# Windowed attention with sinks and an MLP on one Trainium2 core: moving four casts and pairing the sink products

## The chip, the core and the metric

The kernel runs on one core of one Trainium2 chip. A core has TensorE (PE, matrix products), VectorE (DVE), ScalarE (ACT), GpSimd (POOL) and SyncE (SP, which only issues transfers here). All five run their own instruction lists in order and wait for one another by semaphores. The metric is device time in microseconds; lower is better. Before the change the median of four runs is 217.16 us (216.92 to 217.25).

## What is computed

Attention over 4 batches of 8 heads, 768 tokens, 64 elements a head, in which a token sees the first four tokens (the sinks) and the last 128; then an MLP with the activation h * sigmoid(1.702 h).

```python
scores = scale * np.matmul(q, k.transpose(0, 1, 3, 2))
is_sink = pos[None, :] < 4
in_window = (rel >= 0) & (rel < 128)
a = softmax(np.where(is_sink | in_window, scores, -1e9))
x = (a @ v).transpose(0, 2, 1, 3).reshape(3072, 512)
h = x @ w_in                     # w_in 512 x 2048
out = (h * (1.0 / (1.0 + np.exp(-1.702 * h)))) @ w_out
```

All inputs and the output are float32; the kernel multiplies in float16.

## The kernel before

**Tiling.** The 3072 tokens are 12 blocks of 256, numbered k = 0 to 11; a batch is three blocks, r = k mod 3. A block is two halves (j) of 128 tokens. The 8 heads are 4 pairs p; i is the head in its pair. Blocks with r > 0 also see the block before them and the sinks.

**Stages of a block.** `load` (L403) brings q, k and v by transfers and casts them to float16 in pieces by `copy` (L294, so all casts and copies have the line L295). `turn` (L506) transposes q and k into `blkT`: blocks 0 to 3 on PE (L542), from block 4 on by a transposing transfer that SP issues (L564). `scores` (L572) multiplies: a group of one pair (blocks 0 and 1) or two pairs (later), each head in a PSUM bank of its own; the first group of a block with r > 0 also makes the scores of the sinks for all four pairs in one more bank (L594). So a group takes 2 to 5 of the 8 banks. In blocks 0 and 1 a matmul with the identity (L606) puts the mask under the scores. ACT takes exps (L639 for the window into `at`, L626 for the sinks into `ats`), DVE multiplies by the mask from block 2 on (L646). `back` (L657) multiplies by v (L679) and leaves sums and products in a bank; v carries a column of ones, so a head has 65 columns. DVE takes reciprocals (L697, rcp) and scales (L701, xn), and x is transposed into `xT`, on PE in blocks 0 to 2 (L725, with a copy by L295), by SP's transfer later (L713). `mm1` (L738) makes the first product of the MLP in 8 steps of two 128-column chunks (L752), each step with tanh on ACT (L764) and one combining instruction on DVE (L766). The second product is L781 in blocks 0 and 1; later blocks use a form with seven block products instead of eight (L947, in the last block L873), for which DVE and POOL make sums and differences of g (L847) and, once, of the weights (L826).

**Who sets the order.** Nothing is ordered by hand. Every step is an `Op` with the engines that may run it, a duration the author assumed, a priority (smaller is more urgent) and the PSUM banks it takes. `Plan.run` (L76) simulates all engines with these and at each step places the operation that can start first, the more urgent one if several can start within 20 ns. The lists that come out are the instruction order of each engine. Priorities follow a nominal timetable, `nominal(k, slot)` (L387), of 17.3 us a block in 8 slots. A step that several engines may run goes to the one that would end it first.

**Around the change.** In `Plan.run`, L122 to L134: an operation that takes more than two banks and can't have them yet sets `held_from`, and operations that take banks and would start after that are put off, so that the waiting group gets its banks. L126 applies only to groups of three banks or more. The casts of v are allowed by `CAST_V` (L363): block 1's may go to POOL, DVE or ACT, blocks 2 and 3's to POOL, from block 4 on to ACT (L366); their priority is `nominal(k - 1, -4)` (L482), for block 1 the value 350. The casts of q and k (L449 to L452) are eight a block from block 4 on, each 64 x 512, all on POOL. In block 0 reciprocal and scaling have the priority -2245 for pair 2 and 2080 for pair 3 (L698, L708), and the copy of the transposed x -1380 and 2945 (L732).

In `av` (L669) the sink product comes first in each head's group of products:

```python
for i in range(2):
    mms = [(As[:, bass.ts(j, P)], vs16[:, b, p, i])] if r else []
    mms += [(A[:, i, c : c + P], src[:, jj, 2 * p + i]) for src, jj, c in blocks]
    for n, (a_, v_) in enumerate(mms):
        nc.tensor.matmul(avp()[:, j, i], a_, v_, start=(n == 0), stop=(n == len(mms) - 1))
```

`As` holds the exps of the sinks of all heads, and `vs16` the sinks' v with zeros in the rows of the other heads; so both heads of a pair have the same left operand there.

Of the kernel before, what the change touches and what calls it, by code (L numbers as in the profile page):

```python
# [14 lines left out]
P = 128  # L15
# [45 lines left out]
class Plan:  # L61
# [14 lines left out]
    def run(self, warm=None, warm_until=0.0, late_bank=0.0):  # L76
# [39 lines left out]
        while todo:  # L116
            best = None
            for e in ENGINES:
                found = sorted(
                    [(*could(o, e), o) for o in ready[e]], key=lambda x: (x[2].prio, x[2].seq)  # L120
                )
                keep, held_from = [], None  # L122
                for s0, s, o in found:
                    if s0 is None:
                        continue
                    if o.acq and o.acq[1] > 2 and (s is None or s > s0):  # L126

                        held_from = s0 if held_from is None else min(held_from, s0)
                        if s is not None:
                            keep.append((s, o))  # L130
                        continue
                    if s is None or (o.acq and held_from is not None and s >= held_from):
                        continue
                    keep.append((s, o))  # L134
                if not keep:
                    continue
                first = min(s for s, _ in keep)
                s, o = min(((s, o) for s, o in keep if s <= first + 20), key=lambda x: (x[1].prio, x[1].seq))
                lat = o.engs[e][1]
                key = s if len(o.engs) == 1 else s + lat - min(x[1] for x in o.engs.values())  # L140
                if best is None or key < best[0]:
                    best = (key, s, o, e)
            if best is None:
                raise RuntimeError("no operation can be planned")
            _, s, o, e = best
            dur, lat = o.engs[e]
            if e == "PE" and warm and s < warm_until:
                t = max(free["PE"], 400.0)
                while t + 300 < s:
                    order.append((t, -1, warm, e, None))  # L150
                    t += 400 if t < 4500 else 220
            for x in o.engs:
                ready[x].remove(o)
            o.eng, o.start = e, s
            if o.acq:
                cls, n = o.acq
                o.banks, o.places = [], []
                for _ in range(n):
                    b = min((b for b in bank_free if bank_free[b] <= s), key=lambda b: (bank_free[b], b))
                    del bank_free[b]  # L160
                    o.banks.append(b)
                    p = min((p for p in count[cls] if count[cls][p] <= s), key=lambda p: (count[cls][p], p))
                    del count[cls][p]
                    o.places.append(p)
            free[e] = s + dur
            if isinstance(lat, tuple):
                ns, nd = lat
                t = s + dur
                while sum(n * min(1.0, (b - t) / max(b - a, 1.0)) for a, b, n in ring[e] if b > t) + nd > RING:
                    t += 25  # L170
                free[e] = t
                soft = e == "POOL"
                begin = max(s + (2200 if soft else 1300), dma_free[soft])
                shared = max(0.0, min(dma_free[not soft] - begin, ns))
                if shared:
                    dma_free[not soft] += shared
                dma_free[soft] = begin + ns + shared
                ring[e].append((begin, dma_free[soft], nd))
                landed[soft].append(dma_free[soft] + 900)
                o.end = dma_free[soft] + 900 + o.late  # L180
            else:
                o.end = s + lat
            for owner, i in o.rel:
                t = o.end + 80
                bank_free[owner.banks[i]] = t
                count[owner.acq[0]][owner.places[i]] = t
            for u in o.users:
                u.left -= 1
                if not u.left:
                    for x in u.engs:  # L190
                        ready[x].append(u)
            order.append((s, o.seq, o.fn, e, o))
            todo -= 1
# [9 lines left out]
def kernel(  # L203
# [11 lines left out]
    nc = tc.nc  # L215
# [6 lines left out]
    NK = B * R  # L222
# [9 lines left out]
    KS, LASTS = globals().get('OPT',{}).get('KS',2), globals().get('OPT',{}).get('LASTS',NK)  # L232
# [19 lines left out]
    vs16 = pool.tile([P, B, NP, 2, E], FP16, name="vs16")  # L252
# [25 lines left out]
    plan = Plan(8, {"m": 1, "s": 5, "t": 4, "a": 2, "x": 2, "h": RTH, "o": OPT_("NO", 3)})  # L278
# [9 lines left out]
    def cast(n, engs):  # L288

        ns = {"POOL": (n / 0.96 + OPT_("PC", 100), n / 0.96 + OPT_("PC", 100) + 100), "DVE": (n / 1.92 + 65, n / 1.92 + 165),  # L290
              "ACT": (n / 1.2 + 100, n / 1.2 + 210)}
        return {e: ns[e] for e in engs.split()}
# [18 lines left out]
    OPT = globals().get("OPT", {})  # L311
# [48 lines left out]

    OPT = globals().get("OPT", {})
    CAST_QK = ["DVE ACT", "POOL DVE"] + ["POOL"] * (NK - 2)
    CAST_V = ["POOL DVE ACT", OPT.get("V1", "POOL DVE ACT")] + ["POOL"] * (NK - 2)  # L363

    for k_ in range(OPT.get("VK", 4), NK):
        CAST_V[k_] = OPT.get("VA", "ACT")  # L366
# [20 lines left out]
    def nominal(k, slot):  # L387
        return 9000.0 + k * L + slot * L / 8
# [14 lines left out]
    def load(k):  # L403
        b, r = divmod(k, R)
        sl = k if k < RS else (k - 1) % (RS - 1)
        t0 = r * TB
        prio = load_at(f"a{k}")
        war = reuse("s32", sl) + ([o_m[k - 2, 0][-1]] if k > KT else [])
        dst, dv = qk32[sl], v32[sl]
        lq = {}  # L410
# [23 lines left out]
        def lv(dma, h):  # L434
# [3 lines left out]
                   prio=load_at("a1") + 1.5 + k / 8 if k < 2 else load_at(f"v{k}") if k == 2 else prio + 0.7, kind="load")]  # L438
# [4 lines left out]
        war = reuse("qk16", k % RQ)  # L443
        if k >= KT:
            C = slots(c16)
            for e in range(2):
                for j in range(2):
                    for i in range(2):
                        def f(eng, e=e, j=j, i=i):  # L449
                            copy(eng, C[64 * i : 64 * i + 64, e, :, j].rearrange("s p (h d) -> s p h d", h=2),  # L450
                                 dst[64 * j : 64 * j + 64, e, :, i].rearrange("s (p h) d -> s p h d", h=2))
                        o = plan.any(cast(512, "ACT" if k > KS and e == j and i < OPT.get("QA", 0) else CAST_QK[k]), f, lq[e] + war, prio=nominal(k - 1, -7), kind="cqk")  # L452
                        o_cqk[k, 2 * e + j, i] = o
        else:
            C = eights(c16)
            for h in range(2):
                for e in range(2):
                    def f(eng, e=e, h=h):
                        copy(eng, C[:, e, :, :, h].rearrange("s i a d -> s a i d"),
                             dst[:, e].rearrange("s h i d -> s (h i d)").rearrange("s (h a i d) -> s h a i d", h=2, a=4, i=2)[:, h])  # L460
                    o_cqk[k, e, h] = plan.any(cast(512, CAST_QK[k] if k != 1 else "DVE ACT" if e else OPT.get("Q1", "POOL")), f, [lq[e][h]] + war,
                                              prio=nominal(k - 1, -7 + 2 * h) if k else NEVER + h, kind="cqk")
# [3 lines left out]
        war = reuse("v16", k % RV)  # L466
# [4 lines left out]
        for n in range(parts):  # L471
            o_l = o_lv[0]
            got = []
            for j in range(2):
                for i in range(2):
# [3 lines left out]
                    if k < 2 and "DVE" in ns:  # L479
                        ns["DVE"] = (60 * w + 70, 60 * w + 170)  # L480
                    o = plan.any(ns, f, [o_l] + war + [o_ones],
                                 prio=(nominal(k - 1, -4) if k else NEVER + 5 + n), kind="cv")  # L482
# [174 lines left out]
    def back(k, p):  # L657

        b, r = divmod(k, R)
# [6 lines left out]
        def avp():  # L666
            return f32(o_a)[:, 0 : 4 * E].rearrange("s (j h e) -> s j h e", j=2, h=2)

        def av():  # L669
            for j in range(2):  # L670
                if r:
                    blocks = [[(vp, 1, 0), (vt, 0, P)], [(vt, 0, 2 * P), (vt, 1, 3 * P)]][j]
                else:
                    blocks = [[(vt, 0, 0)], [(vt, 0, P), (vt, 1, 2 * P)]][j]
                for i in range(2):
                    mms = [(As[:, bass.ts(j, P)], vs16[:, b, p, i])] if r else []
                    mms += [(A[:, i, c : c + P], src[:, jj, 2 * p + i]) for src, jj, c in blocks]
                    for n, (a_, v_) in enumerate(mms):
                        nc.tensor.matmul(avp()[:, j, i], a_, v_, start=(n == 0), stop=(n == len(mms) - 1))  # L679

        dur = 12 * 31 if r else 6 * 31
        deps = [*o_m[k, p], *o_cv[k, p]] + ([o_se[k], *o_cv[k - 1, p], o_vs[b]] if r else [])
        rc, X = rcp[u % RR], xn[u % RR]
        if k < KX:
# [1 line left out]
        else:  # L686
# [3 lines left out]
            war = []  # L690
# [422 lines left out]
```

## Time and profile before

| | |
|---|---|
| median of the runs | 217.16 us (216.92 to 217.25) |
| the profiled execution | 216.79 us, of which the span of instructions is 215.0 us |
| TensorE clock granted | 1.00 throughout |
| busy in the span | PE 206.8, DVE 172.1, ACT 146.1, POOL 100.2 us |
| casts of v on ACT | 38, of them 35 of 64 x 512, mean 619 ns |
| casts of q and k on POOL, 64 x 512 | 64, mean 646 ns |
| matmuls of L679 with `at` and `v` / with `ats` and `vs` | 352 / 128, all of 65 columns |

Times are us unless marked ns. "PE" is the matmul, "PEld" its weight load, which overlaps. A line of a group gives line, engine, operation, tiles (out<-in) and shapes, then busy time and the mean of one. In an order of time, the columns are start, length, engine, line and operation, and in brackets how long the engine stood before it and what ended that. A duration of a matmul holds its way through the array; the next one starts well before it ends, so the distance of starts tells what a matmul costs when they follow closely.

### The profile page before, as it was taken

Reading aid. Unit: us, or ns where it says so; the run is one execution under the profiler, and the core shown is the slowest. Engines: PE = TensorE matmul, PEld = TensorE weight load, DVE = VectorE, ACT = ScalarE, POOL = GpSimd, SP = SyncE. Lnnn points to the kernel's source line nnn. Section 1 sums busy time; section 2 is a strip of 40 time slices with the busy share of each in tenths; the row PEclk is TensorE's granted clock in tenths of the full one; section 3 lists DMA queues with packets and bytes.
Section 4 is the critical chain, followed back from the end, with each engine's and each line's share of the span. In section 5 each row is a group of like instructions: output and inputs, shape, how many; then the busy total and the mean of one; then the engine's idle time right before and its main releaser. Section 6 shows DMA issues by size and latency. Waiting matters only on the chain.

```text
span 215.0 us, 5827 instructions
## 1 busy us (share of the span) xinstructions
PE 206.8 (96%) x2290; PEld 166.6 (78%) x2290; DVE 172.1 (80%) x369; ACT 146.1 (68%) x290; POOL 100.2 (47%) x144
## 2 busy tenths in 40 slices
PE   7979999999999999999999999999999999999992
PEld 2447876676767878988988978988988988988881
DVE  3685777997779798889878989889878969978861
ACT  2699645957987768769696597679696566525530
POOL 3496437799862482196712393196702202203210
PEclk9999999999999999999999999999999999999999
DMA  5999999999959728989979729959894024024044
GB/s 183 352 234 204 207 304 210 324 297 283 206 128 224 190 49 125 266 163 281 173 157 214 198 54 194 267 137 272 162 147 102 3 51 98 0 56 94 0 99 99
DMA packets 65914, 36.58 MB, mean 170 GB/s; under 512 B 27968, under 2 KB 61120, under 8 KB 65888
## 3 DMA queue, kind: packets, MB, share of 16 engines
q1 hardware_dynamic: 60848, 30.19, 59.7%
q0 software_dynamic: 4592, 5.37, 13.2%
q10 hardware_dynamic: 448, 0.66, 1.0%
q8 instruction: 18, 0.29, 0.6%
q14 instruction: 8, 0.07, 0.1%
HBM read 27.56 MB, written 6.29 MB: 157 GB/s over the span
## 4 chain that ended last, share of the span: by engine, by line
PE 77%; DVE 11%; ACT 7%; issue 3%; ACTq 0%; DVEq 0%
PE bank L752 34%; PE bank L947 19%; PE bank L781 6%; PE bank L679 6%; PE bank L614 4%; DVE gT L766 3%; DVE gF L847 3%; ACT at L639 3%; PE bank L873 3%; PE bank L1061 3%; ACT v L295 2%; PE bank L542 2%; DVE xb L701 1%; DVE at L646 1%; ACT th L764 1%
## 5 line engine op out<-in xcount | busy, mean ns | idle before, releaser
L752 PE MATMUL bank<-xT,w_in 128*128 128x256 f16 x768 | 99.7, 273 | 0.4 <-DVE gT L766 0.4
L764 ACT ACTIVATE th<-bank 128x512 f16<-128x512 f32 x96 | 57.3, 601 | 40.9 <-PE bank L752 32.6
L752 PEld LDWEIGHTS <-w_in 128*128 128x128 f16 x768 | 72.0, 98 | 11.5 <-issue 2.5
L766 DVE SCALAR_TENSOR_TENSOR gT<-th,bank 128x512 f16<-128x512 f16 x96 | 65.3, 682 | 14.2 <-ACT th L764 12.4
L847 POOL TENSOR_TENSOR gT<-gT 128x512 f16<-128x512 f16 (+1 forms) x22 | 24.8, 1128 | 73.1 <-DVE gF L847 66.1
L639 ACT ACTIVATE at<-bank 128x512 f16<-128x512 f32 (+1 forms) x96 | 49.2, 571 | 6.1 <-PE bank L614 6.0
L295 POOL CAST qk<-qk 64x512 f16<-64x512 f32 (+1 forms) x70 | 44.9, 643 | 13.9 <-DMA qk<-in_q_dram 11.3
L947 PE MATMUL bank<-third,gF 128*128 128x256 f16 x144 | 34.1, 273 | 0.0
L947 PE MATMUL bank<-w_out,gT 128*128 128x256 f16 x144 | 34.0, 273 | 0.0
L947 PEld LDWEIGHTS <-gT 128*128 128x128 f16 x288 | 27.5, 98 | 4.1 <-issue 0.9
L646 DVE TENSOR_TENSOR at<-at,bank 128x1024 f16<-128x1024 f16 (+1 forms) x40 | 25.4, 637 | 6.2 <-ACT at L639 6.0
L947 PE MATMUL bank<-wf,gT 128*128 128x256 f16 x144 | 27.0, 272 | 0.0
L295 ACT CAST v<-v 64x512 f16<-64x512 f32 (+1 forms) x38 | 22.9, 603 | 1.0 <-DMA v<-in_v_dram 0.3
L947 PEld LDWEIGHTS <-gF 128*128 128x128 f16 x216 | 21.1, 98 | 2.6 <-DVE gF L847 0.2
L679 PE MATMUL bank<-v,at 128*128 128x65 f16 x352 | 21.2, 193 | 0.6 <-DVE at L646 0.3
L679 PEld LDWEIGHTS <-at 128*128 128x128 f16 x352 | 17.6, 97 | 1.6 <-DVE at L646 0.5
L947 PE MATMUL bank<-w_out,gF 128*128 128x256 f16 x72 | 17.2, 273 | 0.0
L781 PE MATMUL bank<-w_out,gT 128*128 128x512 f16 x64 | 15.9, 379 | 0.0
L701 DVE TENSOR_TENSOR xb<-bank,rcp 128x256 f16<-128x256 f32 x36 | 15.0, 417 | 0.4
L679 PE MATMUL bank<-vs,ats 128*128 128x65 f16 x128 | 14.9, 193 | 0.1
L847 DVE TENSOR_TENSOR gF<-gT,gF 128x512 f16<-128x512 f16 (+1 forms) x22 | 14.1, 639 | 0.3
L614 PEld LDWEIGHTS <-blkT 64*128 64x128 f16 x256 | 8.0, 94 | 8.0 <-issue 6.2
(75 smaller groups left out, 208.9 us busy)
## 6 DMA issues: line engine op xcount, KB each, us to landing
out_dram<-osb SPq DMA_DIRECT2D x46, 128.0 KB, 2.4
v<-in_v_dram SPq DMA_DIRECT2D x11, 512.0 KB, 6.6
qk<-in_q_dram SPq DMA_DIRECT2D x8, 512.0 KB, 4.6
qk<-in_k_dram SPq DMA_DIRECT2D x8, 512.0 KB, 6.0
w_in<-in_moe_w_in_dram POOLq DMA_DIRECT2D x4, 512.0 KB, 9.3
w_out<-in_moe_w_out_dram POOLq DMA_DIRECT2D x4, 512.0 KB, 12.4
qk<-in_q_dram SPq DMA_DIRECT2D x6, 256.0 KB, 5.1
qk<-in_k_dram SPq DMA_DIRECT2D x4, 256.0 KB, 4.9
```

Source lines behind the costliest of these rows:

```text
L295: {"POOL": nc.gpsimd.tensor_copy, "DVE": nc.vector.tensor_copy, "ACT": nc.scalar.copy}[e](out=out, in_=in_)
L614: nc.tensor.matmul(f32(o_s, 2 * n + i)[:, c : c + w], src[d, j], Q[d].rearrange("d j s -> d (j s)")[:, q0 : q0 + w], start=k >= KM, stop=T ...
L639: nc.scalar.activation(out=A[:, i, 0:W], in_=f32(o_s, 2 * n + i)[:, 0:W], func=AF.Exp, scale=scale)
L646: nc.vector.tensor_tensor(out=A[:, :, 0:W], in0=A[:, :, 0:W], in1=mask(c0, c0 + W).unsqueeze(1).to_broadcast((P, 2, W)), op=ALU.mult,)
L679: nc.tensor.matmul(avp()[:, j, i], a_, v_, start=(n == 0), stop=(n == len(mms) - 1))
L701: nc.vector.tensor_tensor(out=X, in0=avp()[:, :, :, 0:D], in1=rc.to_broadcast((P, 2, 2, D)), op=ALU.mult)
L752: nc.tensor.matmul(f32(holder[0])[:, bass.ts(e, TB)], w_in16[:, c, bass.ts(Fi, P)], X[:, c] if k < KX else X2[:, :, c], start=(c == 0), st ...
L764: o_t = op("ACT", 490, 610, lambda first=first: nc.scalar.activation(out=th[first.places[0]], in_=f32(first), func=AF.Tanh, scale=0.851), ...
L766: o_g[k, s] = op("DVE", 604, 710, lambda first=first, s=s: nc.vector.scalar_tensor_tensor(out=g[:, 2 * s : 2 * s + 2].rearrange("p a t -> ...
L781: nc.tensor.matmul(f32(holder[0])[:, 0:w], g[:, Fi, bass.ts(j, P)], w_out16[:, Fi, c0:c1], start=(Fi == 0), stop=(Fi == NF - 1),)
L847: (nc.gpsimd if eng == "POOL" else nc.vector).tensor_tensor(out=o_, in0=a, in1=b_, op=what)
L947: nc.tensor.matmul(f32(holder[0])[:, bass.ts(half, N)], lhs, rhs, start=fresh and s == 0 and half == what(0)[0][0], stop=s == NS - 1, skip ...
```

## The change

Four edits. The planner: a group that would wait, while one that can start no later already waits, is not considered at all in that step. Block 1's casts of v: DVE only. From block 4 on, two of a block's eight casts of q and k (q with j = 0, i = 0 and k with j = 1, i = 0) go to ACT instead of POOL. And in blocks with r > 0, one matmul of 130 columns per half makes the sink products of both heads of a pair, and the window's products are added to it.

```diff
@@ Plan.run
                     if o.acq and o.acq[1] > 2 and (s is None or s > s0):
-
+                        if held_from is not None and s0 >= held_from:
+                            continue
                         held_from = s0 if held_from is None else min(held_from, s0)
...
     CAST_QK = ["DVE ACT", "POOL DVE"] + ["POOL"] * (NK - 2)
-    CAST_V = ["POOL DVE ACT", OPT.get("V1", "POOL DVE ACT")] + ["POOL"] * (NK - 2)
+    CAST_V = ["POOL DVE ACT", OPT.get("V1", "DVE")] + ["POOL"] * (NK - 2)
...
-                        o = plan.any(cast(512, "ACT" if k > KS and e == j and i < OPT.get("QA", 0) else CAST_QK[k]), f, lq[e] + war, prio=nominal(k - 1, -7), kind="cqk")
+                        o = plan.any(cast(512, "ACT" if k > KS and e == j and i < OPT.get("QA", 1) else CAST_QK[k]), f, lq[e] + war, prio=nominal(k - 1, -7), kind="cqk")
...
@@ av
             for j in range(2):
                 if r:
+                    nc.tensor.matmul(avp()[:, j], As[:, bass.ts(j, P)], vs16[:, b, p], start=True, stop=False, skip_group_check=True)
                     blocks = [[(vp, 1, 0), (vt, 0, P)], [(vt, 0, 2 * P), (vt, 1, 3 * P)]][j]
                 else:
                     blocks = [[(vt, 0, 0)], [(vt, 0, P), (vt, 1, 2 * P)]][j]
                 for i in range(2):
-                    mms = [(As[:, bass.ts(j, P)], vs16[:, b, p, i])] if r else []
-                    mms += [(A[:, i, c : c + P], src[:, jj, 2 * p + i]) for src, jj, c in blocks]
-                    for n, (a_, v_) in enumerate(mms):
-                        nc.tensor.matmul(avp()[:, j, i], a_, v_, start=(n == 0), stop=(n == len(mms) - 1))
-
-        dur = 12 * 31 if r else 6 * 31
+                    for n, (src, jj, c) in enumerate(blocks):
+                        nc.tensor.matmul(
+                            avp()[:, j, i], A[:, i, c : c + P], src[:, jj, 2 * p + i],
+                            start=not r and n == 0, stop=n == len(blocks) - 1, **(dict(skip_group_check=True) if r else {}),
+                        )
+
+        dur = 8 * 31 + 2 * 57 if r else 6 * 31
```

## The prediction

> **What bounds the kernel now.** I read the page first, then the stretches, then the waits of PE, then the order of each engine where PE stands still.
>
> ```profile
> PE 206.8 (96%) x2290; PEld 166.6 (78%) x2290; DVE 172.1 (80%) x369; ACT 146.1 (68%) x290; POOL 100.2 (47%) x144
> ...
> PE 77%; DVE 11%; ACT 7%; issue 3%; ACTq 0%; DVEq 0%
> ```
>
> PE is busy 206.8 of 215.0 us and carries 77% of the chain that ended last. So time can only be won where PE stands still, or from the matmuls themselves. The stretches say where that is (columns: length, then busy time of PE, PEld, DVE, ACT, POOL, granted clock, DMA):
>
> ```profile
> 10.00:15.00 5.00, 4.26 (x60) 2.49 (x59) 4.25 (x13) 4.89 (x13) 4.63 (x11) 1.00 1.17 245
> 15.00:20.00 5.00, 4.44 (x64) 2.81 (x64) 2.58 (x11) 4.86 (x11) 4.14 (x8) 1.00 1.24 206
> ...
> 40.00:64.00 24.00, 23.96 (x259) 17.20 (x257) 19.52 (x47) 19.45 (x38) 20.27 (x32) 1.00 0.93 240
> ...
> 79.20:94.00 14.80, 14.80 (x186) 12.72 (x187) 13.05 (x28) 10.76 (x22) 6.13 (x9) 1.00 0.86 180
> 94.00:110.10 16.10, 15.84 (x173) 13.66 (x172) 13.90 (x29) 13.84 (x28) 11.12 (x16) 1.00 0.92 191
> ...
> 141.90:157.90 16.00, 15.81 (x170) 13.66 (x169) 13.89 (x29) 13.78 (x28) 11.11 (x16) 1.00 0.89 192
> ```
>
> PE is idle 1.3 us between 10 and 20 us, with ACT full (9.75 of 10). After 20 us it hardly stops, but DVE is at 81 to 88%, and ACT at 86% in the stretches 94 to 110 and 141.9 to 157.9, each of which holds the casts of two blocks. Busy rows contain the drain of a matmul, so I also took the starts: distance from one matmul to the next, less the usual distance of that shape (29 ns at 65 columns, 56 at 128, 109 at 256, 216 at 512). The excess is 3.0 us from 10 to 20 us and 6.9 us after it; of the latter only six pieces are over 0.2 us (0.25 at 63.7, 0.50 at 66.6, 0.39 at 78.7, 0.42 at 100.8, 0.52 at 126.0, 0.35 at 148.7: 2.4 us).
>
> The start, ACT and DVE in order of time:
>
> ```profile
> 13.51 0.91 ACT L639 ACTIVATE at<-bank 128x384 f16<-128x384 f32 x2
> 14.44 1.88 ACT L295 CAST v<-v 64x512 f16<-64x512 f32 x3
> 16.34 2.06 ACT L639 ACTIVATE at<-bank 128x512 f16<-128x512 f32 x4
> 18.27 0.42 ACT L626 ACTIVATE ats<-bank 128x256 f16<-128x256 f32 x1
> ...
> 14.45 0.67 DVE L295 CAST v<-v 64x512 f16<-64x512 f32 x1
> ...
> 16.91 0.49 DVE L295 COPY xT<-bank 128x256 f16<-128x256 f16 x2 [0.39 <-PE bank L725]
> 19.32 0.18 DVE L697 RECIPROCAL rcp<-bank 128x4 f32<-128x4 f32 x1 [1.93 <-PE bank L679]
> ```
>
> Of the four casts of block 1's v, three stand on ACT ahead of block 1's exps; the scores of its first group were there at 14.3. The exps of the sinks end at 18.7, and only then can the products L679 of block 1 begin. DVE is idle 0.39 + 1.93 us meanwhile.
>
> **Sink products.** 32 groups (8 blocks with sinks, 4 head pairs). Before: 12 matmuls of 65 columns, 12 x 29.5 = 354 ns. After: 8 of 65 and 2 of 130, 236 + 2 x 57 = 350 ns, 57 taken a little over the 56 at 128 columns. So 4 to 5 ns a group, 0.15 us, all on PE's path. [...] I take 0.15 us. The 64 weight loads that go (97 ns each in the rows) lie under the matmuls. The first matmul of a group needs `ats` before and after, so no wait moves.
>
> **Second v cast.** ACT loses 3 x 0.62 = 1.88 us on its chain, DVE gains 3 x 0.665 = 2.0 us. DVE's queue in the plan puts rcp, xn and xT copies of pairs 0 to 2 of block 0 ahead of these casts, and those of pair 3 behind them (priorities 2080 and 2945 against 350). So I expect on DVE: cast, two xT copies, rcp and xn of pair 2, the other casts up to about 18.1 to 18.4, then rcp, xn and the copy of pair 3 near 19.3. Two things follow. Gain: exps of block 1 start near 14.5 instead of 16.3, free two banks 1.9 us earlier, and the sinks' exps end near 18.1. PE's excess from 14.3 to 18.7 is 0.13 + 0.71 + 0.11 + 0.23 = 1.2 us; the 0.71 waits for a bank held until the xT copy of DVE ends (15.4), the 0.23 for the sinks' exps. Loss: first L752 of block 0 needs all four xT copies and goes from 18.06 to about 19.3. What covers it is the last score group of block 1 (0.85 us, before at 22.25) and two groups of L679 (0.36 each). If that cover is not there, PE stands up to 1.2 us longer. Bounds: -1.1 and +1.2 us. I take -0.5: all of the 0.23 and 0.3 of the 0.71, since the bank comes from an exp at about 15.1 instead of the copy. v had landed before either engine took it, so DVE waits for no transfer.
>
> [...]
>
> **One q and one k cast by ACT.** For blocks 4 to 11, two of eight casts: 16 x 0.646 = 10.3 us leave POOL. No row shows such a cast on ACT; the nearest is ACT's v cast of the same 64x512 shape, 0.619 us: 16 x 0.62 = 9.9 us onto ACT, 1.24 us a block of about 15.9 us. What waits behind: on ACT, tanh L764 and exp L639, and behind these DVE's L766 and PE's h banks. If a cast were queued before its load lands, all of these stand; the 38 v casts on ACT lost only 0.3 us to that, so the planned landing is late enough. On SP the transpose L564 follows the last cast; it can go up to 1.3 us sooner, with the loads and stores around it in SP's order. That buys little: the transposed tiles that the trace times landed 3 to 12 us before their scores, and PE has no wait for them. POOL's casts do lengthen DVE's differences L847 (0.64 to 0.71 against 0.42 us, some six of them), so a quarter fewer casts return under 0.5 us of DVE. Cover for 1.24 us a block: ACT idles 4.0 us in the single-block stretch 79 to 94 and 2.3 us in the double stretch 94 to 110, where 2.5 us come. Bounds: -0.5 us (DVE and the early transpose close the gaps at 63.7 and 126) and +3.7 us (half of the 2.5 us in each of three double stretches, counting 50 to 64). I take -0.2, nearest to the ordinary stretches, where PE did not stop although ACT was 73% busy.
>
> **One waiting score group.** From block 2 on, PE ran the groups of every block in order, pairs 0-1 before 2-3 and no group of a later block ahead (starts 37.3, 40.4, 49.4, 53.4, 64.1, 69.7 and so on to 180.4). The old rule already let the first waiting group hold back smaller ones, so the new line takes away only a choice that was not used: 0. It matters only if the other edits reorder the plan.
>
> Sum: -0.15 - 0.5 - 0.2 = -0.85 us. The profiled execution took 216.79 us (span 215.0 and 1.8 around it), so 215.9; the median of the runs is 0.37 above it: 216.3.
>
> **Rivals.** *The wait only changes engine (same).* DVE's casts delay the fourth xT copy and PE loses what ACT gave back; ACT's cover suffices: 217.16 - 0.15 = 217.0. For it: the 0.71 us gap already waited for DVE. Against: DVE's 2.3 us of idle time there. *ACT becomes the bound in the double stretches (slower).* With 4 x 0.62 us there, 13.8 becomes 16.3 of 16.1 us; tanh comes late, L766 with it, and PE meets the h banks. It decides from where less than about half of ACT's idle 2.3 us can be used. At 0.8 us in each of three stretches: 2.4 us, less the 0.65 of the first two edits: 218.9. For it: DVE waited 12.4 us for ACT's tanh already, and the planner counts 490 ns for a tanh that takes 601. Against: PE has the L947 products to fill in. *The change is as good as nothing* because a planner reorders everything by a few ns: some tenths either way, within the first two cases.
>
> **Numbers.** 216.3 with chance 0.50; unchanged 0.18; slower 0.32. 0.2% (0.43 us) is about what can be told from no change. Range 214.9 (start bound of -1.1, half of the six large gaps closed) to 218.9.
>
> **What would show it.** Right: ACT's exps of block 1 start near 14.5; L679's first sink row at or before 18.4; PE busy 10 to 20 us above 8.7; PE busy 94 to 110 not under 15.8. Wrong: L752 starting after 19.5 with PE idle before it; ACT over 15.5 us busy in 94 to 110 with PE waits for L766 or L764; an ACT cast waiting for in_q or in_k.

## The result and the profile after

The changed kernel takes 216.18 us in the median of 35 runs (215.53 to 217.39), the kernel before 217.07 us in 54; the ratio is 0.997 with a 95% interval of 0.996 to 0.9979, so about 0.65 us are gained (0.45 to 0.87). The medians lie 0.89 us apart, the means 0.65. The forecast was 216.3 us and a gain of 0.85 us. The profiled execution took 215.68 us with a span of 213.9 us (before 216.79 and 215.0); it is the third fastest of the 35.

The first lines of the changed kernel's page, engines and chain:

```profile
PE 206.2 (96%) x2226; PEld 166.4 (78%) x2226; DVE 172.7 (81%) x374; ACT 152.6 (71%) x302; POOL 88.2 (41%) x127
...
PE 75%; ACT 10%; DVE 8%; issue 2%; DMA 2%; SPq 0%; ACTq 0%; DVEq 0%
```

PE is still the bound. ACT is busy 6.5 us longer and POOL 12 us less: the casts moved, and with them a few other steps to which the plan gave another engine. PE's last matmul starts at 209.71 us instead of 210.45, that is 0.74 us sooner; the other 0.32 us of the span lie behind it, in the last transfers, which the change does not touch: from the issue of the last two stores (L908, now L911) to the end of the span it took 4.19 us before and 3.88 us now.

The changed kernel's stretches (columns as before), start and the two that I had called double:

```profile
10.00:15.00 5.00, 4.32 (x64) 2.52 (x62) 4.21 (x15) 4.91 (x14) 4.69 (x9) 1.00 1.13 238
15.00:20.00 5.00, 5.00 (x68) 3.04 (x68) 4.09 (x14) 4.05 (x9) 4.66 (x9) 1.00 1.24 207
94.00:110.00 16.00, 15.81 (x174) 13.56 (x173) 14.15 (x29) 12.84 (x27) 6.81 (x9) 1.00 0.94 197
142.00:158.00 16.00, 15.81 (x175) 13.57 (x174) 14.05 (x29) 12.73 (x26) 8.21 (x11) 1.00 0.84 191
```

From 15 to 20 us PE is now full (4.44 before), and DVE has taken over what ACT gave up. In the two later stretches ACT has not filled up: it is less busy than before (12.84 us of 16.0 against 13.84 of 16.1). The plan put the casts at other times, and ACT is fuller there: from 50 to 60 us it is busy 9.83 us (9.23 before), from 40 to 180 us 115.5 us (105.7 before). So these two stretches no longer test whether ACT becomes the bound. In excess of starts, PE lost 3.04 us from 10 to 20 us before and loses 2.46 us now; after 20 us it is 6.9 us in both.

The start, in the changed kernel's order of time: ACT, DVE, then PE.

```profile
13.48 1.40 ACT L640 ACTIVATE at<-bank 128x384 f16<-128x384 f32 x3
14.80 0.37 ACT L296 COPY xT<-bank 128x256 f16<-128x256 f16 x1
15.07 0.60 ACT L640 ACTIVATE at<-bank 128x512 f16<-128x512 f32 x1
...
17.09 0.39 ACT L627 ACTIVATE ats<-bank 128x256 f16<-128x256 f32 x1
...
14.34 0.48 DVE L296 CAST v<-v 64x512 f16<-64x512 f32 x1
14.74 0.27 DVE L296 COPY xT<-bank 128x256 f16<-128x256 f16 x1
14.95 0.16 DVE L700 RECIPROCAL rcp<-bank 128x4 f32<-128x4 f32 x1
15.14 0.42 DVE L296 CAST v<-v 64x512 f16<-64x512 f32 x1
15.59 0.42 DVE L704 TENSOR_TENSOR xn<-bank,rcp 128x256 f16<-128x256 f32 x1
16.05 0.96 DVE L296 CAST v<-v 64x512 f16<-64x512 f32 x2
...
14.92 0.29 PE L595 MATMUL bank<-blkT,ks 128*32 128x256 f16 x4
...
18.37 0.22 PE L673 MATMUL bank<-vs,ats 128*128 128x130 f16 x1
...
19.08 1.04 PE L755 MATMUL bank<-xT,w_in 128*128 128x256 f16 x8
```

This is the chain that the forecast described: exps of block 1 follow block 0's at once (the third of the three from 13.48), the sinks' exps end at 17.5 instead of 18.7, the group with sinks starts at 14.92 instead of 15.49, and the first L755 (before: L752) starts at 19.08, a microsecond later than before, behind a last score group and two groups of products. A DVE cast of v takes 0.42 to 0.52 us, not the 0.665 of the one row of before.

### The profile page after: what moved, and what is told of

Read it like the earlier page. It is cut to its first block, busy times and chain, and to the rows that moved or that the text cites. A ratio compares the mean times of both kernels' runs of the same rounds, so it can differ in the third digit from the quotient of the medians.

```text
span 213.9 us, 5716 instructions
## 1 busy us (share of the span) xinstructions
PE 206.2 (96%) x2226; PEld 166.4 (78%) x2226; DVE 172.7 (81%) x374; ACT 152.6 (71%) x302; POOL 88.2 (41%) x127
## 4 chain that ended last, share of the span: by engine, by line
PE 75%; ACT 10%; DVE 8%; issue 2%; DMA 2%; SPq 0%; ACTq 0%; DVEq 0%
PE bank L755 32%; PE bank L950 21%; PE bank L784 5%; PE bank L615 4%; PE bank L679 4%; DVE gT L769 4%; ACT v L296 3%; PE bank L876 3%; ACT at L640 3%; ACT th L767 3%; DMA qk<-in_q_dram 2%; DVE gF L850 1%; PE bank L673 1%; PE bank L607 1%; PE bank L543 1%
## 5 line engine op out<-in xcount | busy, mean ns | idle before, releaser
L755 PE MATMUL bank<-xT,w_in 128*128 128x256 f16 x768 | 99.7, 273 | 1.3 <-DVE gT L769 1.3
L755 PEld LDWEIGHTS <-w_in 128*128 128x128 f16 x768 | 72.3, 98 | 12.0 <-issue 2.8
L850 POOL TENSOR_TENSOR gT<-gT 128x512 f16<-128x512 f16 (+1 forms) x22 | 25.0, 1137 | 79.9 <-DVE gF L850 61.2
L640 ACT ACTIVATE at<-bank 128x512 f16<-128x512 f32 (+1 forms) x96 | 48.5, 571 | 5.5 <-PE bank L615 5.4
L296 POOL CAST qk<-qk 64x512 f16<-64x512 f32 (+1 forms) x54 | 33.8, 629 | 21.0 <-DMA qk<-in_q_dram 14.5
L950 PE MATMUL bank<-third,gF 128*128 128x256 f16 x144 | 34.0, 273 | 0.0
L950 PE MATMUL bank<-w_out,gT 128*128 128x256 f16 x144 | 33.6, 273 | 0.0
L950 PEld LDWEIGHTS <-gT 128*128 128x128 f16 x288 | 27.5, 98 | 4.1 <-issue 0.9
L950 PE MATMUL bank<-wf,gT 128*128 128x256 f16 x144 | 26.9, 272 | 0.0
L950 PEld LDWEIGHTS <-gF 128*128 128x128 f16 x216 | 21.0, 98 | 2.6 <-issue 0.2
L296 ACT CAST v<-v 64x512 f16<-64x512 f32 (+1 forms) x35 | 21.0, 601 | 0.7
L679 PE MATMUL bank<-v,at 128*128 128x65 f16 x352 | 20.0, 193 | 0.3 <-POOL v L296 0.3
L679 PEld LDWEIGHTS <-at 128*128 128x128 f16 x352 | 17.2, 98 | 1.5 <-issue 0.4
L950 PE MATMUL bank<-w_out,gF 128*128 128x256 f16 x72 | 17.1, 273 | 0.0
L850 DVE TENSOR_TENSOR gF<-gF,gT 128x512 f16<-128x512 f16 (+1 forms) x22 | 13.8, 628 | 0.4
L615 PE MATMUL bank<-blkT 64*128 64x256 f16 x192 | 13.5, 244 | 0.0
```

The costliest lines, as they stand in the source:

```text
L296: {"POOL": nc.gpsimd.tensor_copy, "DVE": nc.vector.tensor_copy, "ACT": nc.scalar.copy}[e](out=out, in_=in_)
L615: nc.tensor.matmul(f32(o_s, 2 * n + i)[:, c : c + w], src[d, j], Q[d].rearrange("d j s -> d (j s)")[:, q0 : q0 + w], start=k >= KM, stop=T ...
L640: nc.scalar.activation(out=A[:, i, 0:W], in_=f32(o_s, 2 * n + i)[:, 0:W], func=AF.Exp, scale=scale)
L679: nc.tensor.matmul(avp()[:, j, i], A[:, i, c : c + P], src[:, jj, 2 * p + i], start=not r and n == 0, stop=n == len(blocks) - 1, **(dict(s ...
L755: nc.tensor.matmul(f32(holder[0])[:, bass.ts(e, TB)], w_in16[:, c, bass.ts(Fi, P)], X[:, c] if k < KX else X2[:, :, c], start=(c == 0), st ...
L850: (nc.gpsimd if eng == "POOL" else nc.vector).tensor_tensor(out=o_, in0=a, in1=b_, op=what)
```

## The experiments

All were run beside the kernel before on the same chip; the ratio is to it, with its 95% interval. "Excess" is PE's, from 10 to 20 us.

| edits | run | ratio | interval | in us | excess |
|---|---|---|---|---|---|
| all four | changed kernel | 0.997 | 0.996 to 0.9979 | -0.65 | 2.46 |
| v casts | only_v | 1.0094 | 1.0062 to 1.0126 | +2.0 | 2.74 |
| v casts, new planner line | v_hold | 1.0034 | 1.0016 to 1.0053 | +0.7 | 2.65 |
| q and k casts | only_q | 0.9998 | 0.9983 to 1.0013 | 0.0 | 3.22 |
| pairing and its duration in the planner | only_s | 1.001 | 0.9995 to 1.0025 | +0.2 | 3.15 |
| pairing, old duration | sink_olddur | 0.9972 | 0.9959 to 0.9985 | -0.6 | 3.03 |
| duration alone | dur_only | 1.0011 | 0.9998 to 1.0025 | +0.2 | 3.29 |
| all without v casts | undo_v | 1.003 | 1.0013 to 1.0046 | +0.65 | 3.26 |
| all without q, k casts | undo_q | 1.0026 | 1.0011 to 1.004 | +0.6 | 2.56 |
| all without pairing | undo_s | 0.9987 | 0.9974 to 0.9999 | -0.3 | 2.56 |
| all, old duration | after_olddur | 0.9965 | 0.995 to 0.9981 | -0.8 | 2.69 |
| v casts moved, order kept | v_fixed | 1.0086 | 1.0055 to 1.0117 | +1.9 | 5.01 |
| q, k casts moved, order kept | q_fixed | 1.0109 | 1.0094 to 1.0125 | +2.4 | 3.24 |

**Block 1's v casts alone.**

```diff
-OPT.get("V1", "POOL DVE ACT")
+OPT.get("V1", "DVE")
```

> The kernel before with one edit: block 1's casts of v on DVE only. My theory (the gain is PE's idle time in the first 20 us): -0.4 to -0.7 us, PE's excess from 10 to 20 us down from 3.0 to about 2.4 us. Rival 1 (the gain is the q and k casts off POOL): within 0.2 us of before. Rival 2 (any reordering of the plan moves the time by some tenths, and the edits do not add up): anything from -0.6 to +0.6 us, with the difference lying after 20 us.

It was 2.0 us slower: all three theories missed the size; the second rival had the place right, after 20 us. The excess of the first 20 us did fall, to 2.74 us (before 3.04). The loss is at 79 us. PE there, and PE's stretches just after (the column behind POOL's is the granted clock):

```profile
78.52 0.23 PE L614 MATMUL bank<-blkT,blkT 64*128 64x128 f16 x2
78.59 0.33 PE L614 MATMUL bank<-blkT 64*128 64x256 f16 x4
78.75 0.22 PE L614 MATMUL bank<-blkT,blkT 64*128 64x128 f16 x2
78.81 0.33 PE L614 MATMUL bank<-blkT 64*128 64x256 f16 x4
81.37 0.29 PE L594 MATMUL bank<-blkT,ks 128*32 128x256 f16 x4 [2.23 <-ACT at L639]
...
82.14 2.06 PE L752 MATMUL bank<-xT,w_in 128*128 128x256 f16 x11
```

```profile
82.00:83.00 1.00, 1.00 (x13) 0.72 (x8) 1.00 (x2) 0.97 (x2) 0.00 (x0) 0.83 1.12 212
83.00:86.00 3.00, 3.00 (x16) 2.07 (x15) 1.12 (x3) 2.95 (x8) 0.38 (x2) 0.50 0.92 199
86.00:90.00 4.00, 4.00 (x55) 3.62 (x54) 3.74 (x11) 2.28 (x6) 1.20 (x2) 0.99 1.03 275
```

The second score group of block 5 (no L594, 4 banks) runs ahead of the first one (L594, 5 banks), takes its banks, and PE stands 2.23 us until ACT has read them. Then, in this execution, the clock is granted at 0.50 for about 3.4 us. That is the order which the new planner line forbids.

**The v casts with the new line.** This is only_v with one line more:

```diff
                     if o.acq and o.acq[1] > 2 and (s is None or s > s0):
+                        if held_from is not None and s0 >= held_from: continue
```

> The kernel before with block 1's casts on DVE and the new line in the planner, nothing else. Alone, the casts made the plan put block 5's second score group ahead of its first, and PE stood 2.2 us for the banks. The new line forbids that order. If that order is what cost 2 us: within 0.6 us of before, either side. If the casts themselves cost it: about +2 us again.

1.0034: about 1.3 us come back, and block 5's first score group is ahead of its second again. It is slightly outside the 0.6 us that I had allowed, and slower than before, although the first 20 us are nearly as good as in the changed kernel (excess 2.65 against 2.46 us). So the line undoes the larger part of what the v casts do to the plan, not all of it. In the kernel before and in the changed kernel it does nothing: planned with it and without it, the instruction lists of all five engines are the same.

**The v casts moved, order kept.** The plan is that of before; at the end, the casts that it gave to ACT are written to DVE.

```diff
-            ins = fn(e)
+            ins = fn(getattr(o, "to", None) or e)      # o.to = "DVE" for block 1's v casts
```

> The kernel before, planned as before, but when the instructions are written out the three ACT casts of block 1's v go to DVE, at the times the plan had for them; every other engine's order is that of before. It shows what the move is worth if nothing else is reordered. DVE then has three casts ahead of the first xT copy. If the move of 1.9 us off ACT is itself the gain: -0.3 us or more. If the gain needs the plan's new order (xT copies between the casts): PE's gap near 14.8 us grows from 0.7 to about 1.3 to 1.6 us, the time is 0 to +0.8 us.

+1.9 us, more than either figure. DVE and PE of this run:

```profile
15.03 1.39 DVE L295 CAST v<-v 64x512 f16<-64x512 f32 x3
16.34 0.46 DVE L295 COPY xT<-bank 128x256 f16<-128x256 f16 x2
...
16.66 0.29 PE L594 MATMUL bank<-blkT,ks 128*32 128x256 f16 x4 [1.02 <-DVE xT L295]
```

Three casts stand ahead of the first xT copy, PE waits for the bank of that copy, and after that and smaller waits around it the granted clock fell here too (0.84 in the stretch 15 to 20 us; of the excess of 5.01 us about 0.8 is the slow clock). That explains the size. Such a stretch of half clock, 3.4 of some 217 us, lowers the mean clock of an execution by about 0.008, and the eight runs fall into two groups: four with a mean clock of 0.989 to 0.992 took 219.9 us in the median, four with 0.995 to 1.000 took 217.9. So the order alone costs 0.9 us, just above what I had allowed for it, and the clock about 1.9 us more in half of the runs. Taking the casts off ACT is not by itself the gain. The planned runs that gain in the first 20 us differ from this one in the order: the plan, knowing of the move, puts an xT copy on ACT and another between the casts.

**The q and k casts alone, planned and with the order kept.**

```diff
-OPT.get("QA", 0)
+OPT.get("QA", 1)
```

> The kernel before with one edit: two of eight casts of q and k a block on ACT from block 4 on. My theory: -0.2 to +0.4 us, the first 20 us as before. Rival 1: -0.6 to -0.9 us, nearly the whole difference. Rival 2: anything within 0.6 us either way.

> The kernel before, planned as before, with the 16 casts of q and k moved from POOL to ACT when the instructions are written out; PE's, DVE's and SP's orders are those of before. My theory: ACT's spare time covers them, within +0.5 us of before. If ACT is the bound in the stretches with casts of two blocks: +1.5 us or more. If POOL's load was what cost time: -0.5 us.

Planned: no difference. With the order kept: +2.4 us, the case I had given as ACT being the bound. It is not ACT's total, 14.3 us busy of 16 between 94 and 110 us; it is what stands behind a cast. ACT, DVE and the wait that PE had three times:

```profile
108.40 0.62 ACT L295 CAST qk<-qk 64x512 f16<-64x512 f32 x1
109.04 1.25 ACT L295 CAST v<-v 64x512 f16<-64x512 f32 x2
110.31 0.60 ACT L764 ACTIVATE th<-bank 128x512 f16<-128x512 f32 x1
110.94 0.62 ACT L295 CAST v<-v 64x512 f16<-64x512 f32 x1
111.46 0.37 ACT L979 ACTIVATE part<-bank 128x256 f32<-128x256 f32 x1
...
111.86 0.69 DVE L980 SCALAR_TENSOR_TENSOR osb<-bank,part 128x512 f32<-128x512 f32 x1 [0.23 <-ACT part L979]
```

```profile
PE bank L594 <- DVE osb L980: 1.4, 3, 0.6
```

In the kernel before, the same part (it started at 108.94 us) and the same wait of PE:

```profile
108.94 0.37 ACT L979 ACTIVATE part<-bank 128x256 f32<-128x256 f32 x1
...
PE bank L594 <- DVE osb L980: 0.6, 2, 0.4
```

The cast pushes a part L979 of the second product back, DVE's L980 needs it and frees the bank late, and the score group waits for the bank. PE's excess after 20 us grows by about 3 us, to 9.8 us. This wait is 1.0 us of it (by starts), and 0.6 us more is a score group that waits for a bank of the second product which ACT itself empties late (L798, at 65.9 us); the rest is in pieces under 0.5 us. With its own plan the same edit loses nothing.

**The pairing alone, with the old and the new duration, and the duration alone.**

```diff
-        dur = 12 * 31 if r else 6 * 31
+        dur = 8 * 31 + 2 * 57 if r else 6 * 31      # dur_only: only this; sink_olddur: all but this
```

> The kernel before with the paired sink products, but the planner still counts the old duration for them, so that it orders everything as before. It measures the matmuls by themselves. My theory: -0.15 us (32 groups, 4 to 5 ns each). [...] Rival 2 expects -0.15 us too, since nothing is reordered.

> The kernel before with one number changed: the duration that the planner counts for a group of products with v in blocks with sinks, 362 instead of 372 ns; the matmuls are as before. Only the order changes. My theory: within 0.3 us of before, either sign. Rival 2: 0.4 us or more either way, as much as the whole change.

> The kernel before with the paired sink products and the planner's new duration for them. If the order does not matter: -0.15 us, as with the old duration. If reordering counts: the sum of the runs with the pairing alone and with the duration alone, whatever that is.

With the order fixed, the pairing gains 0.28% (0.6 us, 0.3 to 0.9). Three more pairs of runs have the same instruction lists on every engine and differ only in the pairing: undo_s and after_olddur (-0.22%), v_hold and undo_q (-0.08%), dur_only and only_s (-0.01%). Each of these is the difference of two ratios to before, good to about 0.2%. The mean of the four is -0.15%, 0.3 us. In the traces a group of products with sinks lasts 364 ns before and 356 ns after in the median, from its first matmul to the next one behind it: 8 ns, not the 4 to 5 I had summed, and 0.26 us for 32 groups, which agrees.

The duration alone, 10 ns in a number the planner uses, gives +0.1% with an interval that just holds zero. The pairing in that order, only_s, is at +0.1% too, where the sum of the two single runs was -0.17%. So in the order that this number caused no gain of the pairing is left to see. How much of the 0.4% between only_s and sink_olddur is the order and how much is noise these runs do not tell.

**The change less one edit, and with the old duration.**

> The changed kernel with block 1's casts of v free to go to any of the three engines again. My theory: it loses most of the gain, 0.4 to 0.7 us slower than the changed kernel, 0.2 to 0.4 us faster than before. Rival 1: as fast as the changed kernel. Rival 2: no relation to what the edit did alone.

> The changed kernel with all casts of q and k on POOL again. My theory: within 0.3 us of the changed kernel, so 0.6 to 1.2 us faster than before. Rival 1: back to within 0.3 us of before. Rival 2: no relation to what the edit did alone.

> The changed kernel with a sink product for each head again, and the planner's old duration. My theory: 0.15 us slower than the changed kernel if order does not matter, within 0.4 us if it does; 0.5 to 0.9 us faster than before.

> The changed kernel, but the planner counts the old duration for the products with v. Its order is that of the changed kernel without the pairing, so against that run it measures the pairing a second time with the order fixed, and it may be the fastest version. Pairing worth 0.15 us by its matmuls: -0.4 us against before. Pairing worth 0.6 us, as it was in before's order: -0.9 us against before.

Without the v casts 1.003, without the q and k casts 1.0026, without the pairing 0.9987. So in company the v casts and the q and k casts are worth about 0.6% each, while alone the v casts cost 0.3% (with the planner's line, as here) and the q and k casts nothing. undo_q has the instruction lists of v_hold, so it is the same order with the pairing. Where it loses, PE in this run and in the changed kernel at the same place:

```profile
78.92 0.29 PE L595 MATMUL bank<-blkT,ks 128*32 128x256 f16 x4 [0.81 <-DVE osb L983]
...
80.58 0.60 PE L755 MATMUL bank<-xT,w_in 128*128 128x256 f16 x4 [0.82 <-DVE gT L769]
```

```profile
78.00 0.29 PE L595 MATMUL bank<-blkT,ks 128*32 128x256 f16 x4
...
79.29 1.03 PE L755 MATMUL bank<-xT,w_in 128*128 128x256 f16 x8 [0.45 <-DVE gT L769]
```

In undo_q the score group is placed straight behind an L755 and waits 0.81 us for a bank that DVE's L983 frees at 78.9; the next L755 waits 0.82 us. In the changed kernel the plan has eight L950 matmuls in between, and DVE's L983 ends at 77.6. after_olddur is 0.35% faster than before, not distinguishable from the changed kernel; against undo_s, whose order it has, it gains the 0.2% named above.

## Why the forecast held, and where its reasons did not

**PE as the bound, gains only from its idle time or its matmuls:** right. The last matmul started 0.74 us sooner in the profiled runs. The excess from 10 to 20 us accounts for 0.58 us and the shorter sink groups for 0.26 us, together 0.1 us more than what moved; after 20 us the excess is the same. So in this one execution the gain lies where the first two terms put it, and the third term, -0.2 us, is not to be seen. All four signs that were to show the forecast right came (exps of block 1 at 14.2 us, the first sink row at 18.37, PE busy 9.3 us from 10 to 20, 15.81 us from 94 to 110), but the last tests nothing, since the plan had moved ACT's casts elsewhere.

**v casts (-0.5 us by the first 20 us):** the stage and size are right. The six runs that planned this edit have an excess of 2.46 to 2.74 us (mean 2.61), the kernel before and the six other runs without it have 3.03 to 3.29 (mean 3.18): 0.57 us, with no overlap. The mechanism as listed (exps, bank, cover by score group and L679) is what the trace shows. What failed is the unsaid step that a gain at 15 us lasts to the end. In v_hold and undo_q it is there and the runs are still slower than before, because the shifted plan puts new waits at 77 to 93 us. I had called reordering worth "some tenths either way"; between plans it was over 1 us. One reading behind this term was wrong as well. The 0.665 us that I counted for a v cast on DVE came from a single row; the four took 0.48, 0.42, 0.43 and 0.52 us, where DVE's six casts of q and k of 512 elements took 0.43 us each. POOL was not held up beside these casts: to issue three weight transfers it took 0.81, 0.79 and 0.75 us, against 0.81, 0.75 and 0.76 before.

**q and k casts (-0.2 us, covered by ACT's spare time):** the sign came true only in company, and for another reason. The edit alone gives 0.0, and forced into an unaware order +2.4 us: the cover is not ACT's idle time but the planner's freedom. The loss mechanism of my slower rival (late tanh, h banks, three double stretches) is not what q_fixed shows either; there the score groups wait for banks of the second product. DVE's relief did not come: 20 of its 66 differences (L850) took over 0.6 us, against 17 of 66 (L847) before. For the earlier transpose no run shows a gain.

**Sink products (-0.15 us):** right mechanism, size too small: 0.26 us by the group's length, 0.3 us in the mean of the four pairs of runs. The term that was off is the 29.5 ns for a matmul of 65 columns: the sinks' own start 30.3 ns apart in the mean, and 4 x 30.3 less 2 x 56.5 is 8 ns a group. With the same columns in sum, each of the two matmuls that go saved 4 ns.

**One waiting group (0):** right for the change as it stands, where it alters no instruction; and the reserve that it matters if other edits reorder the plan is what only_v and v_hold show, at 1.3 us.

So the sum came out right, in part by luck, for its terms do not stand for separate gains that any plan would have kept: the single edits with the planner's line for the v casts give +0.34, -0.02 and +0.10%, together +0.42%, and the whole change gives -0.30%. The 0.7% between, 1.6 us, is interaction: each edit also changes the plan, and the plan for all of them is none of the single ones. Why the plan with both kinds of casts is the good one is open: I can name the waits it avoids at 78 to 81 us, but no run shows a rule that would have told so beforehand.

## What to carry to other kernels

Where a planner writes the order, test an edit twice, with its new plan and with the old order kept: the first mixes the edit with a reshuffle, which here was worth as much as the edits. The second can mislead too, where the old order does not suit the edit (v_fixed, q_fixed). An engine's spare time did not cover a moved step where what was queued behind that step frees somebody's buffer (q_fixed, +2.4 us). And an order rule that changes no instruction today can still be what makes the next edit safe.

## What the hardware showed that I had not expected

A stand of TensorE of 2.23 us (only_v), or one of 1.02 us with smaller waits around it (v_fixed; PE was busy for 1.7 of the 3 us from 15 to 18 us), was followed in the profiled executions by 3.4 us at a granted clock of 0.50. The low clock began there only when PE was at work again (in only_v at 82.7 us, 1.3 us after the stand had ended; in v_fixed at 18.4 us, 1.8 us after). The eleven matmuls of L752 there lasted 2.06 us, where eight start within 0.87 us otherwise. So in these executions the stand was paid for a second time: 3.4 us at half the clock are about 1.7 us of work, and the two groups of v_fixed lie 1.9 us apart.

It did not happen in every execution. Only one execution of a run has a trace; the mean clock of the others tells it as an estimate. It is 0.988 to 0.992 in four of six runs of only_v and four of eight of v_fixed, the two with the traced stretches among them, in two of 22 of undo_q, one of twelve of v_hold and one run of the kernel before (218.04 us), and 0.995 or more in all others. What came before the low clock in the last three is not shown. The waits of 0.81 and 0.82 us in the profiled execution of undo_q left the clock at 1.00, as did those of up to 0.55 us after the start in that of the kernel before. Even without the low clock only_v is slower than before: its two runs at a mean clock of 1.000 took 217.87 and 219.37 us.
